# A spectral layer and an FFN: turning the first token block on PE instead of by DMA transposes, and a re-pipelined LayerNorm start

## The chip, the cores and the metric

The kernel runs on one core of a Trainium2 chip. The metric is the device time of one execution in microseconds (us). The engines are PE (TensorE, matmul; PEld is its weight load), DVE (VectorE), ACT (ScalarE), POOL (GpSimd) and SP (SyncE, which here issues DMAs). A profiled execution has a span, from its first to its last instruction; the time of the same execution is about 2 us longer.

## The reference, cut to what matters

```python
x = A_x                                              # 2048 tokens x 576
h  = x + irfft2(rfft2(layernorm(x)) * (w_r + 1j*w_i))  # A: spectral layer
h2 = h + (gelu(n @ w_gate) * (n @ w_up)) @ w_down      # B: FFN, n = layernorm(h), 4608 wide
```

## The kernel before

The kernel writes the transforms as matmuls with tables and goes through four parts: the start (LN1 and the first token transform), a loop of 16 steps (stages D, B and V: channel transform, product with W, and the way back), the inverse stage (I and N per token tile, residual, sums for LN2), and the FFN in four blocks of 512 tokens. gate/up contracts over 576 channels as 9 pieces of 64; gate uses rows 0 to 63 of the array and up rows 64 to 127 at the same time (the traces show about twice the columns per us: 648 matmuls of 512 columns in 70.1 us, where 10 of 289 columns that use all rows take 1.34 us). So it needs the normalised tokens turned (channels on partitions), with each 64-channel piece in both halves. Before, HN holds each piece twice, and nine 128x128 DMA transposes per token tile make HT from it.

A small recording layer takes operations in program order, each engine's list in order, and puts in the waits. In the traces here an engine (and the SP queue) stands at an operation that has to wait and does not go past it: in the run turn_dma20 below, the queue stands from 96.02 to 99.17 us before two copies.

```python
    # start: four rounds q of four token tiles; EPT is the epsilon tile
    P.op(POOL, lambda g: g.memset(EPT[:, :], EPS), w=["EPT"])   # stands behind 9 W loads on POOL
    def ln1_stats(q):
        ...  # 3 tiles by bn_stats on DVE, 1 tile by two ACT passes; sqrt on ACT (needs EPT), reciprocal on DVE
        for c in range(4 * q, 4 * q + 4):
            P.op(DVE, lambda v, c=c: v.tensor_scalar(ATS[:, c, :], ATB[:, c, :], RS1[:, c:c + 1], None, op0=ALU.mult), ...)
    for q in range(4):
        ln1_stats(q)
        for dt in range(5):
            a_mm(q, dt)
            if q >= 1:
                a_ev(q - 1, dt)          # odd dt on DVE, even dt on ACT
    ...
    def prep(c):                          # normalise tile c and turn it
        hs = c % 2                        # HN has two buffers
        for i in range(2):                # the 576 channels twice, in 64-wide pieces
            P.op(DVE, lambda v, ...: v.tensor_scalar(HN[:, hs, :, i, :], x9, TM[:, 1, c:c + 1], RS2[:, c:c + 1], ...), ...)
        for k in range(9):
            P.dma(SP, HT[:, k, 128 * (c % 4):128 * (c % 4) + 128], HN[:, hs, k, :, :]..., transpose=True)
    for c in range(NT + 1):               # inverse stage
        if c < NT: st_I(c)                # 10 matmuls
        if c >= 1: st_N(c - 1)            # 2 matmuls; residual on DVE, squares on ACT
        if c in (5, 9, 13): ln2((c - 5) // 4)
        if 5 <= c < 9: prep(c - 5)        # the first FFN block
    ...
    for tb in range(4):
        for f in range(36):
            gu(36 * tb + f, tb, f)        # 18 matmuls
            if tb < 3 and f % 4 == 3 and f < 16:
                prep(4 * (tb + 1) + f // 4)
        for p in range(4): down(tb, p)
```

Of the kernel before, what the change touches and what calls it, by code (L numbers as in the profile page):

```python
# [14 lines left out]
NG = 16  # L15
# [14 lines left out]
def build_tables():  # L30
# [95 lines left out]
    dt_[4, 64:96] = N[256:288]  # L126
    T["DTAB"] = dt_.transpose(1, 0, 2).reshape(128, -1)
# [154 lines left out]
def _build(nc, A_x, A_w_r, A_w_i, B_w_gate, B_w_up, B_w_down, out):  # L282
# [10 lines left out]
    HN = sb.alloc("HN", [128, 2, 9, 2, 64], BF16)  # L293
# [58 lines left out]

    P.op(POOL, lambda g: g.memset(WS[:, :, :, K2:KW], 0.0), w=["Wz"])
    xv = A_x[0].rearrange("(p c) d -> p c d", c=NT)
    ov = out[0].rearrange("(p c) d -> p c d", c=NT)
    for q in range(4):
        P.dma(SP, XO[:, 4 * q:4 * q + 4, :], xv[:, 4 * q:4 * q + 4, :], f"x{q}", w=[("X", c) for c in range(4 * q, 4 * q + 4)])
# [5 lines left out]
    for pl, src in ((0, A_w_r), (1, A_w_i)):  # L363
        eng = (SP, POOL)[pl]
        P.op(eng, None, r=[("X", 4)])
        for jj in range(4):
            a = bass.AP(src.tensor, 16 * jj * K2, [[128 * K2, 16], [K2, NG], [1, K2]])
            P.dma(eng, WS[jj:64:4, :, pl, 0:K2], a, f"w{pl}", r=["Wz"], w=[("W", pl, jj)])
            a = bass.AP(src.tensor, (64 + 16 * jj + 15) * K2, [[128 * K2, 16], [-K2, NG - 1], [1, K2]])
            P.dma(eng, WS[64 + jj:128:4, 1:NG, pl, 0:K2], a, f"w{pl}", r=["Wz"], w=[("W", pl, 4 + jj)])  # L370
        a = bass.AP(src.tensor, 64 * K2, [[128 * K2, 16], [16 * K2, 4], [1, K2]])
        P.dma(eng, WS[64:128, 0, pl, 0:K2], a, f"w{pl}", r=["Wz"], w=[("W", pl, 8)])
# [3 lines left out]
    P.dma(SP, IT[:, :, :].rearrange("p a b -> p (a b)"), dram["ITAB"][:, :], "it", w=["IT"])  # L376

    P.op(POOL, lambda g: g.memset(EPT[:, :], EPS), w=["EPT"])
    P.op(POOL, lambda g: g.memset(U[64:128, 4, :, :, :], 0.0), w=["Uz"])
# [4 lines left out]
    def ln1_stats(q):  # L384
        for c in range(4 * q, 4 * q + 4):
            if c % 4 == 3:
# [4 lines left out]
                continue  # L391
            for h in range(2):
                P.op(DVE, lambda v, c=c, h=h: v.bn_stats(ST1[:, c, h, :], XO[:, c, 288 * h:288 * h + 288]), r=[("X", c)], w=[("ST1", c, h)])  # L393
        for c in range(4 * q, 4 * q + 4):
            if c % 4 == 3:
# [4 lines left out]
            else:  # L400
                P.op(DVE, lambda v, c=c: v.bn_aggr(MV1[:, c, :], ST1[:, c, :, :]), r=[("ST1", c, 0), ("ST1", c, 1)], w=[("MV1", c)])
        cs = slice(4 * q, 4 * q + 4)
        P.op(ACT, lambda a, cs=cs: a.activation(RS1[:, cs], MV1[:, cs, 1], ACTF.Sqrt, bias=EPT[:, 0:1]),
             r=[("MV1", c) for c in range(4 * q, 4 * q + 4)] + ["EPT"], w=[("SD1", q)])
        P.op(DVE, lambda v, cs=cs: v.reciprocal(RS1[:, cs], RS1[:, cs]), r=[("SD1", q)], w=[("RS1", q)])
        for c in range(4 * q, 4 * q + 4):
            P.op(DVE, lambda v, c=c: v.tensor_scalar(ATS[:, c, :], ATB[:, c, :], RS1[:, c:c + 1], None, op0=ALU.mult),  # L407
                 r=[("RS1", q), "ATB"], w=[("ATS", c)])
# [10 lines left out]
    def a_ev(q, dt):  # L419
# [4 lines left out]
        if dt % 2 == 1:  # L424
# [4 lines left out]
    for q in range(4):  # L429
        ln1_stats(q)  # L430
        for dt in range(5):
            a_mm(q, dt)
            if q >= 1:
                a_ev(q - 1, dt)
    for dt in range(5):
        a_ev(3, dt)
# [77 lines left out]
    P.alias(["FT", "BT", "VT"], [("HT", 0, i) for i in range(4)])  # L514
# [14 lines left out]
    def st_N(c):  # L529
        sl = c % 2  # L530
        for h in range(2):
            b = 4 + 2 * sl + h
# [3 lines left out]
        P.op(DVE, lambda v, sl=sl, x2=x2, c=c: v.scalar_tensor_tensor(x2, banks(4 + 2 * sl, 2, 288), 1.0, x2, op0=ALU.mult, op1=ALU.add,  # L536
                                                                      accum_out=SB2[:, 0, c:c + 1]),
             r=[("PS", 4 + 2 * sl), ("PS", 5 + 2 * sl)], w=[("X", c), ("S0", c)])
# [3 lines left out]
    def ln2(q):  # L542
# [5 lines left out]
             r=[("M2", q)] + [("S1", c) for c in rr], w=[("V2", q)])  # L548
        P.op(ACT, lambda a, cs=cs: a.activation(RS2[:, cs], RS2[:, cs], ACTF.Sqrt, bias=EPT[:, 0:1]), r=[("V2", q), "EPT"], w=[("SD2", q)])
        P.op(DVE, lambda v, cs=cs: v.reciprocal(RS2[:, cs], RS2[:, cs]), r=[("SD2", q)], w=[("RS2", q)])  # L550

    def prep(c):
        hs = c % 2
        q = c // 4
        x9 = XO[:, c, :].rearrange("p (k e) -> p k e", e=64)
        for i in range(2):
            P.op(DVE, lambda v, c=c, hs=hs, i=i, x9=x9: v.tensor_scalar(HN[:, hs, :, i, :], x9, TM[:, 1, c:c + 1], RS2[:, c:c + 1],  # L557
                                                                        op0=ALU.subtract, op1=ALU.mult),
                 r=[("X", c), ("MN", q), ("RS2", q)], w=[("HN", hs, i)])
        HT = HTS[q % 2]  # L560
        for k in range(9):
            P.dma(SP, HT[:, k, 128 * (c % 4):128 * (c % 4) + 128], HN[:, hs, k, :, :].rearrange("p a b -> p (a b)"), f"tr{c}",
                  r=[("HN", hs, 0), ("HN", hs, 1)], w=[("HT", q % 2, c % 4)] if k == 8 else [("HTp", q % 2, c % 4, k)], transpose=True)

    for c in range(NT + 1):
        if c < NT:
# [3 lines left out]
        if c in (5, 9, 13):  # L570
            ln2((c - 5) // 4)
        if 5 <= c < 9:
            prep(c - 5)
    ln2(3)
# [80 lines left out]
```

## Time and profile before

The time is 569.71 us (median of four runs, 567.68 to 570.77). The profiled span is 565.9 us.

| part | from, us | length, us | bound by |
|---|---|---|---|
| start | 0 | 33.6 | DVE, after a late first round |
| D/B/V loop | 33.58 | 46.1 | PE |
| inverse stage and hand-over | 79.67 | 59.4 | the DMA transposes of the first block |
| FFN | 139.10 | 426.8 | PE |

These are three rows of the slice view of the kernel before: 40 slices of 14.1 us, each digit a busy share in tenths; PEclk is the clock granted to TensorE.

```profile
PE   0579987262999999999999999999999999999998
PEclk9999999556999999999999999999999999999999
DMA  8979998111011100001110000011100000000000
```

PE is full from the eleventh slice on. Before that lie a slow start and a hole in slices 8 to 10, where the granted clock is down to 0.5 and 0.6 as well (half clock, for short). The chain of waits of the same kernel says what held each (start in us, length, then engine, what it wrote, source line and number of instructions):

```profile
8.22 5.15 POOL WS L192 x9
...
13.56 1.28 ACT L403
14.85 0.31 ACT RS_55 L403
...
29.92 0.27 DVE ATS L407
30.23 2.63 PE PS L415 x20
...
33.58 4.99 PE PS L447 x20
...
79.67 2.61 PE PS L524 x20
...
111.87 1.23 SPq L190
113.15 2.33 DMA HT_68<-HN
...
129.51 9.59 issue
139.10 71.39 PE PS L590 x648
```

The first square root (L403) waits until 13.56 us, because EPT comes after nine W loads on POOL; the 1.28 us then are the load of its ACT table, and the square root itself follows at 14.85 us. In the hand-over the chain is the SP queue (SPq L190): 36 transposes, one every 1.27 us. The last 9.59 us are put down to "issue"; the gate/up matmuls (L590) then start when the last transposes have landed. The view by windows of the same stretch (busy us and, in brackets, instructions of each engine, then granted clock, DMA share and GB/s) shows PE starving:

```profile
core 0: us, PE busy (x) PEld busy (x) DVE busy (x) ACT busy (x) POOL busy (x), PEclk, DMA share, GB/s
90.00:100.00 10.00, 5.85 (x45) 4.00 (x43) 3.54 (x9) 3.36 (x9) 0.00 (x0) 1.00 0.73 237
100.00:110.00 10.00, 2.84 (x12) 1.64 (x12) 1.73 (x4) 1.31 (x3) 0.00 (x0) 0.54 0.13 26
110.00:120.00 10.00, 1.41 (x7) 0.74 (x7) 3.45 (x11) 2.38 (x7) 0.00 (x0) 0.50 0.13 28
120.00:130.00 10.00, 8.39 (x48) 5.47 (x46) 4.27 (x15) 6.65 (x16) 0.00 (x0) 0.77 0.11 23
130.00:140.00 10.00, 0.90 (x6) 0.43 (x8) 0.99 (x6) 2.36 (x4) 0.00 (x0) 0.58 0.11 23
```

The DMA share there is 0.11 to 0.13. The transposes load the engines little; they come slowly one after another.

### The profile page before, as it was taken

The page shows a single profiled execution, that of the slowest core. Times are in us where ns is not written, and L with a number is a line of the kernel's source. Part 1 is how long each engine was busy: PE and PEld are TensorE (multiplying, and loading weights), DVE is VectorE, ACT ScalarE, POOL GpSimd, SP SyncE. Part 2 cuts the span into 40 slices and gives each one's busy share as a digit, 9 for nine tenths or more (in the row PEclk, how much of TensorE's full clock was granted, in tenths as well). Part 3 has the DMA queues.
Part 4 walks back from the last instruction along what each step waited for, and adds up shares of the span by engine and source line. Part 5 has one row for each costly group of instructions (what it writes and reads, how often), then busy time and mean ns, then how long its engine had stood idle before and what let it go on. Part 6 is the DMA issues. An engine that isn't in the chain of part 4 may idle for free.

```text
span 565.9 us, 10092 instructions
## 1 busy us (share of the span) xinstructions
PE 506.5 (90%) x4368; PEld 300.5 (53%) x4368; DVE 192.8 (34%) x440; ACT 149.8 (26%) x279; POOL 27.7 (5%) x45
## 2 busy tenths in 40 slices
PE   0579987262999999999999999999999999999998
PEld 0457765141555557754444677444447754444676
DVE  1857754141444330025433210444330023333200
ACT  2545655043223220012233100332220012332100
POOL 4180040000000000000000000000000000000000
PEclk9999999556999999999999999999999999999999
DMA  8979998111011100001110000011100000000000
GB/s 316 230 169 221 222 237 294 26 26 21 8 27 27 25 4 17 17 12 22 24 27 15 6 17 22 11 24 27 24 3 17 17 12 1 1 2 1 6 21 17
DMA packets 35916, 31.37 MB, mean 55 GB/s; under 512 B 24433, under 2 KB 30705, under 8 KB 35873
## 3 DMA queue, kind: packets, MB, share of 16 engines
q0 software_dynamic: 4592, 17.11, 12.6%
q1 hardware_dynamic: 31136, 13.11, 9.0%
q8 instruction: 34, 0.56, 0.4%
q10 hardware_dynamic: 144, 0.52, 0.3%
q14 instruction: 10, 0.07, 0.0%
HBM read 23.64 MB, written 2.36 MB: 46 GB/s over the span
## 4 chain that ended last, share of the span: by engine, by line
PE 79%; SPq 7%; DVE 5%; issue 3%; DMA 2%; ACT 2%; POOL 1%; DVEq 0%; ACTq 0%
PE PS L590 44%; PE PS L603 25%; SPq L190 7%; PE PS L447 4%; PE PS L524 2%; PE PS L461 1%; DMA XO<-in_A_x_dram 1%; DVE ST_52 L393 1%; PE PS L480 1%; POOL WS L192 1%; DMA HT_68<-HN 1%; DVE XO L536 1%; DVE HN L557 1%; ACT SQ L539 1%; PE PS L533 1%
## 5 line engine op out<-in xcount | busy, mean ns | idle before, releaser
L594 ACT ACTIVATE GL<-PS 128x512 bf16<-128x512 f32 x144 | 86.0, 597 | 309.6 <-PE PS L590 306.4
L595 DVE TENSOR_TENSOR AT<-GL,PS 128x512 bf16<-128x512 bf16 x144 | 98.8, 687 | 174.6 <-ACT GL L594 174.4
L590 PE MATMUL PS<-HT_68,WGU 64*128 64x512 bf16 x1296 | 141.9, 378 | 9.8 <-issue 9.6
L603 PE MATMUL PS<-WD,AT 128*128 128x288 bf16 x1152 | 141.8, 286 | 0.0
L590 PE MATMUL PS<-HT_82,WGU 64*128 64x512 bf16 x1296 | 140.6, 376 | 0.1
L603 PEld LDWEIGHTS PS<-WD,AT 128*128 128x128 bf16 x1152 | 112.4, 98 | 29.9 <-issue 1.7
L590 PEld LDWEIGHTS PS<-HT_68,WGU 64*128 64x128 bf16 x1296 | 67.1, 95 | 84.1 <-issue 11.6
L590 PEld LDWEIGHTS PS<-HT_82,WGU 64*128 64x128 bf16 x1296 | 62.8, 94 | 77.4 <-DVE AT L595 0.6
L606 DVE TENSOR_TENSOR OS<-PS,XO 128x288 bf16<-128x288 f32 x32 | 14.6, 458 | 123.9 <-PE PS L603 123.9
L415 PE MATMUL PS<-ATS,XO 128*128 128x128 bf16 (+1 forms) x80 | 10.4, 309 | 22.5 <-DVE ATS L407 22.5
L557 DVE TENSOR_SCALAR HN<-XO,TM,RS_58 128x576 bf16<-128x576 bf16 x32 | 16.8, 567 | 28.5 <-DMA HT_68<-HN 23.0
L533 PE MATMUL PS<-GS,IT 128*128 128x288 bf16 x32 | 7.4, 318 | 21.0 <-ACT GS L526 21.0
L524 PE MATMUL PS<-DT,V 128*128 128x288 bf16 x160 | 25.7, 316 | 0.5 <-ACT V L487 0.5
L447 PE MATMUL PS<-FT,U 128*128 128x289 bf16 x160 | 24.7, 307 | 0.7 <-ACT U L427 0.7
L415 PEld LDWEIGHTS PS<-ATS,XO 128*128 128x128 bf16 (+1 forms) x80 | 8.0, 141 | 24.6 <-DVE ATS L407 23.2
L524 PEld LDWEIGHTS PS<-DT,V 128*128 128x128 bf16 x160 | 17.2, 108 | 6.5 <-issue 0.6
L447 PEld LDWEIGHTS PS<-FT,U 128*128 128x128 bf16 x160 | 15.4, 103 | 6.9 <-issue 0.9
L539 ACT ACTIVATE SQ<-XO 128x576 bf16<-128x576 bf16 x16 | 10.9, 681 | 26.0 <-DVE XO L536 26.0
L536 DVE SCALAR_TENSOR_TENSOR XO<-PS,XO 128x576 bf16<-128x576 f32 x16 | 12.0, 751 | 11.4 <-PE PS L533 11.4
L533 PEld LDWEIGHTS PS<-GS,IT 128*128 128x128 bf16 x32 | 3.0, 106 | 23.6 <-ACT GS L526 22.8
L480 PE MATMUL PS<-VT,ZS 128*128 128x256 bf16 x64 | 9.6, 271 | 2.1 <-DVE ZS L471 1.3
L393 DVE BATCH_NORM_STATS2 ST_52<-XO 128x6 f32<-128x288 bf16 x24 | 9.0, 445 | 6.5 <-DMA XO<-in_A_x_dram 6.5
(50 smaller groups left out, 170.1 us busy)
## 6 DMA issues: line engine op xcount, KB each, us to landing
WGU<-in_B_w_gate_dram POOLq DMA_DIRECT2D x9, 576.0 KB, 22.2
WGU<-in_B_w_up_dram POOLq DMA_DIRECT2D x9, 576.0 KB, 24.1
WD<-in_B_w_down_dram POOLq DMA_DIRECT2D x9, 576.0 KB, 10.5
XO<-in_A_x_dram SPq DMA_DIRECT2D x4, 576.0 KB, 7.2
out_dram<-OS SPq DMA_DIRECT2D x32, 72.0 KB, 1.6
HT_68<-HN SPq DMA_TRANSPOSE x72, 2.4
HT_82<-HN SPq DMA_TRANSPOSE x72, 2.4
FT<-c_ftab SPq DMA_DIRECT2D x1, 725.0 KB, 9.6
```

The source lines that it names most:

```text
L190: fn = lambda e: e.dma_start(out_ap, in_ap, transpose=True)
L415: P.op(PE, lambda t, b=b, w=w, i=i, c=c, dt=dt: t.matmul(bank(b, 0, w, 128 * i, 128 * i + 128), XO[:, c, 128 * dt:128 * dt + w], ATS[:, c, ...
L447: P.op(PE, lambda t, b=b, o=o, dt=dt, g=g: t.matmul(bank(b, 0, 128, 0, K2), U[:, dt, g, :, :], FT[:, dt, o, 0:K2], start=(dt == 0), stop=( ...
L524: P.op(PE, lambda t, b=b, h=h, kt=kt, c=c: t.matmul(bank(b, 0, 128, 0, 288), V[:, kt, c, :, :], DT[:, kt, 288 * h:288 * h + 288], start=(k ...
L533: P.op(PE, lambda t, b=b, h=h, c=c, sl=sl: t.matmul(bank(b, 0, 128, 0, 288), IT[:, c, :], GS[:, sl, 288 * h:288 * h + 288], start=True, st ...
L536: P.op(DVE, lambda v, sl=sl, x2=x2, c=c: v.scalar_tensor_tensor(x2, banks(4 + 2 * sl, 2, 288), 1.0, x2, op0=ALU.mult, op1=ALU.add, accum_o ...
L539: P.op(ACT, lambda a, sl=sl, c=c: a.activation(SQ[:, sl, :], XO[:, c, :], ACTF.Square, accum_out=SB2[:, 1, c:c + 1]), r=[("X", c)], w=[("S ...
L557: P.op(DVE, lambda v, c=c, hs=hs, i=i, x9=x9: v.tensor_scalar(HN[:, hs, :, i, :], x9, TM[:, 1, c:c + 1], RS2[:, c:c + 1], op0=ALU.subtract ...
L590: P.op(PE, lambda t, o=o, h0=h0, kt=kt, f=f, b0=b0, HT=HT: t.matmul(bank(b0 + o), WGU[h0:h0 + 64, kt, 128 * f:128 * f + 128], HT[h0:h0 + 6 ...
L594: P.op(ACT, lambda a, s2=s2, b0=b0: a.activation(GL[:, s2, :], bank(b0), ACTF.Gelu_apprx_tanh), r=[("PS", b0)], w=[("GL", s2)])
L595: P.op(DVE, lambda v, s2=s2, b0=b0, f=f: v.tensor_tensor(AT[:, f, :], GL[:, s2, :], bank(b0 + 1), op=ALU.mult), r=[("GL", s2), ("PS", b0 + ...
L603: P.op(PE, lambda t, b0=b0, h=h, f=f, p=p: t.matmul(bank(b0 + h, 0, 128, 0, 288), AT[:, f, 128 * p:128 * p + 128], WD[:, f, 288 * h:288 * ...
```

## The change

There are two intents. In the inverse stage, the first block is turned by five PE matmuls per tile with an identity matrix, copied out of PSUM by DVE, and the other four slots are filled by two half-shifted SBUF copies by DMA. HN now holds each piece once, plus one repeated piece. In the start, the LN1 statistics, the scaling (now one operation on POOL per round) and the PSUM evacuations are spread over DVE, ACT and POOL, EPT is set first, x comes in smaller pieces, and all W loads move to SP. Blocks 2 to 4 of the FFN keep their DMA transposes.

```diff
-    HN = sb.alloc("HN", [128, 2, 9, 2, 64], BF16)
+    HN = sb.alloc("HN", [128, 2, 640], BF16)
+    IDT = sb.alloc("IDT", [128, 128], BF16)
...
+    P.op(POOL, lambda g: g.memset(EPT[:, :], EPS), w=["EPT"])          # now first on POOL
-    for q in range(4):                                                 # x in 4 pieces
+    for i, (c0, c1) in enumerate(((0, 2), (2, 4), (4, 8), (8, 12), (12, 16))):
-        eng = (SP, POOL)[pl]                                           # W loads
+            P.dma(SP, WS[jj:64:4, :, pl, 0:K2], a, f"w{pl}", ...)
...
-        for c in range(4 * q, 4 * q + 4):
-            P.op(DVE, lambda v, c=c: v.tensor_scalar(ATS[:, c, :], ATB[:, c, :], RS1[:, c:c + 1], ...
+        P.op(POOL, lambda g, cs=cs: g.tensor_tensor(ATS[:, cs, :], ATB[:, cs, :], RS1[:, cs].unsqueeze(2).to_broadcast([128, 4, 128]), op=ALU.mult), ...
...
+    ln1_act(0); ln1_stats(0); ln1_sqrt(0)                              # one per line in the kernel
+    ln1_act(1); ln1_stats(1); ln1_scale(0); ln1_sqrt(1)
+    a_quad(0, (ACT, ACT, ACT, ACT, ACT))                               # matmuls and evacuations
+    ln1_act(2); ln1_stats(2); ln1_scale(1); ln1_sqrt(2)
+    a_quad(1, (ACT, ACT, DVE, ACT, DVE))
+    ln1_act(3); ln1_stats(3); ln1_scale(2); ln1_sqrt(3)
+    a_quad(2, (ACT, DVE, ACT, DVE, DVE))
+    ln1_scale(3)
+    a_quad(3, (ACT, DVE, ACT, DVE, ACT))
...
+    def turn_pe(c):
+        for k in range(5):
+            P.op(PE, ... t.matmul(bank(b, 0, 128, o, o + 128), HN[:, hs, 128 * k:128 * k + 128], IDT[:, :], start=True, stop=True), ...)
+        P.op(DVE, ... v.tensor_copy(HT0[:, 0:5, t0:t1], PS[:, 6 * 512:6 * 512 + 640]...), ...)
+        P.dma(SP, HT0[0:64, 5:9, t0:t1], HT0[64:128, 0:4, t0:t1], f"tr{c}", ...)
+        P.dma(SP, HT0[64:128, 5:9, t0:t1], HT0[0:64, 1:5, t0:t1], f"tr{c}", ...)
...
-        if 5 <= c < 9:
-            prep(c - 5)
+        if c in (6, 8, 10, 12):
+            norm((c - 6) // 2)
+        if c in (7, 9, 11, 13):
+            turn_pe((c - 7) // 2)
...
+    GT = (0, 5, 1, 6, 2, 7, 3, 8, 4)      # slot of piece kt for gate
+    UT = (4, 0, 5, 1, 6, 2, 7, 3, 8)      # and for up
```

N uses one pair of PSUM banks in place of two, since banks 6 and 7 now take the turned tiles, and the steps of LN2 are spread over neighbouring tiles (cut here). a_quad(q, engines) is the five matmuls of a round with their evacuations, one engine named for each.

More of the change, by code (lines that the diff above doesn't have):

```diff
@@ L126, in build_tables @@
     dt_[4, 64:96] = N[256:288]
+    T["EYE"] = np.eye(128)
     T["DTAB"] = dt_.transpose(1, 0, 2).reshape(128, -1)
@@ L350, in banks @@
         return PS[:, b * 512:(b + n) * 512].rearrange("p (a c) -> p a c", a=n)[:, :, 0:w]
+    P.op(POOL, lambda g: g.memset(EPT[:, :], EPS), w=["EPT"])
     P.op(POOL, lambda g: g.memset(WS[:, :, :, K2:KW], 0.0), w=["Wz"])
+    P.op(POOL, lambda g: g.memset(U[64:128, 4, :, :, :], 0.0), w=["Uz"])
     xv = A_x[0].rearrange("(p c) d -> p c d", c=NT)
     ov = out[0].rearrange("(p c) d -> p c d", c=NT)
-    for q in range(4):
-        P.dma(SP, XO[:, 4 * q:4 * q + 4, :], xv[:, 4 * q:4 * q + 4, :], f"x{q}", w=[("X", c) for c in range(4 * q, 4 * q + 4)])
+    for i, (c0, c1) in enumerate(((0, 2), (2, 4), (4, 8), (8, 12), (12, 16))):
+        P.dma(SP, XO[:, c0:c1, :], xv[:, c0:c1, :], f"x{i}", w=[("X", c) for c in range(c0, c1)])
     P.dma(ACT, ATB[:, :, :].rearrange("p a b -> p (a b)"), dram["ATAB"][:, :], "atb", w=["ATB"])
@@ L363, in _build @@
     for pl, src in ((0, A_w_r), (1, A_w_i)):
-        eng = (SP, POOL)[pl]
-        P.op(eng, None, r=[("X", 4)])
         for jj in range(4):
             a = bass.AP(src.tensor, 16 * jj * K2, [[128 * K2, 16], [K2, NG], [1, K2]])
-            P.dma(eng, WS[jj:64:4, :, pl, 0:K2], a, f"w{pl}", r=["Wz"], w=[("W", pl, jj)])
+            P.dma(SP, WS[jj:64:4, :, pl, 0:K2], a, f"w{pl}", r=["Wz"], w=[("W", pl, jj)])
             a = bass.AP(src.tensor, (64 + 16 * jj + 15) * K2, [[128 * K2, 16], [-K2, NG - 1], [1, K2]])
-            P.dma(eng, WS[64 + jj:128:4, 1:NG, pl, 0:K2], a, f"w{pl}", r=["Wz"], w=[("W", pl, 4 + jj)])
+            P.dma(SP, WS[64 + jj:128:4, 1:NG, pl, 0:K2], a, f"w{pl}", r=["Wz"], w=[("W", pl, 4 + jj)])
         a = bass.AP(src.tensor, 64 * K2, [[128 * K2, 16], [16 * K2, 4], [1, K2]])
-        P.dma(eng, WS[64:128, 0, pl, 0:K2], a, f"w{pl}", r=["Wz"], w=[("W", pl, 8)])
+        P.dma(SP, WS[64:128, 0, pl, 0:K2], a, f"w{pl}", r=["Wz"], w=[("W", pl, 8)])
     GORD = list(range(1, NG)) + [0]
@@ L376, in _build, with ln1_act @@
     P.dma(SP, IT[:, :, :].rearrange("p a b -> p (a b)"), dram["ITAB"][:, :], "it", w=["IT"])
-    P.op(POOL, lambda g: g.memset(EPT[:, :], EPS), w=["EPT"])
-    P.op(POOL, lambda g: g.memset(U[64:128, 4, :, :, :], 0.0), w=["Uz"])
+    P.dma(SP, IDT[:, :], dram["EYE"][:, :], "eye", w=["IDT"])
     P.op(POOL, lambda g: g.memset(YS[:, :, :, K2:KW], 0.0), w=["Yz"])
     P.op(POOL, lambda g: g.memset(ZS[:, :, :, K2:ZW], 0.0), w=["Zz"])
-    def ln1_stats(q):
+    ACT_TILES = (1, 5, 9, 13)
+    def ln1_act(q):
         for c in range(4 * q, 4 * q + 4):
-            if c % 4 == 3:
+            if c in ACT_TILES:
                 P.op(ACT, lambda a, c=c: a.activation(JNK[:, 0, :], XO[:, c, :], ACTF.Identity, accum_out=SA[:, 0, c:c + 1]),
@@ L390, in ln1_stats @@
                      r=[("X", c)], w=[("SA1", c), "J1"])
-                continue
-            for h in range(2):
-                P.op(DVE, lambda v, c=c, h=h: v.bn_stats(ST1[:, c, h, :], XO[:, c, 288 * h:288 * h + 288]), r=[("X", c)], w=[("ST1", c, h)])
+    def ln1_stats(q):
         for c in range(4 * q, 4 * q + 4):
-            if c % 4 == 3:
+            if c not in ACT_TILES:
+                for h in range(2):
+                    P.op(DVE, lambda v, c=c, h=h: v.bn_stats(ST1[:, c, h, :], XO[:, c, 288 * h:288 * h + 288]), r=[("X", c)], w=[("ST1", c, h)])
+        for c in range(4 * q, 4 * q + 4):
+            if c not in ACT_TILES:
+                P.op(DVE, lambda v, c=c: v.bn_aggr(MV1[:, c, :], ST1[:, c, :, :]), r=[("ST1", c, 0), ("ST1", c, 1)], w=[("MV1", c)])
+        for c in range(4 * q, 4 * q + 4):
+            if c in ACT_TILES:
                 P.op(DVE, lambda v, c=c: v.scalar_tensor_tensor(TM[:, 0, c:c + 1], SA[:, 0, c:c + 1], 1.0 / (D * D), SA[:, 0, c:c + 1],
@@ L399, in ln1_stats, with ln1_sqrt @@
                                                                 op0=ALU.mult, op1=ALU.subtract), r=[("SA1", c), ("TM", c)], w=[("MV1", c)])
-            else:
-                P.op(DVE, lambda v, c=c: v.bn_aggr(MV1[:, c, :], ST1[:, c, :, :]), r=[("ST1", c, 0), ("ST1", c, 1)], w=[("MV1", c)])
+    def ln1_sqrt(q):
         cs = slice(4 * q, 4 * q + 4)
@@ L404, in ln1_stats, with ln1_scale @@
              r=[("MV1", c) for c in range(4 * q, 4 * q + 4)] + ["EPT"], w=[("SD1", q)])
+    def ln1_scale(q):
+        cs = slice(4 * q, 4 * q + 4)
         P.op(DVE, lambda v, cs=cs: v.reciprocal(RS1[:, cs], RS1[:, cs]), r=[("SD1", q)], w=[("RS1", q)])
-        for c in range(4 * q, 4 * q + 4):
-            P.op(DVE, lambda v, c=c: v.tensor_scalar(ATS[:, c, :], ATB[:, c, :], RS1[:, c:c + 1], None, op0=ALU.mult),
-                 r=[("RS1", q), "ATB"], w=[("ATS", c)])
+        P.op(POOL, lambda g, cs=cs: g.tensor_tensor(ATS[:, cs, :], ATB[:, cs, :], RS1[:, cs].unsqueeze(2).to_broadcast([128, 4, 128]), op=ALU.mult),
+             r=[("RS1", q), "ATB"], w=[("ATS", c) for c in range(4 * q, 4 * q + 4)])
     def a_mm(q, dt):
@@ L417, in a_mm, with a_ev @@
                  r=[("X", c), ("ATS", c)], w=[("PS", b)])
-    def a_ev(q, dt):
+    def a_ev(q, dt, eng):
         b = (5 * q + dt) % 8
@@ L423, in a_ev @@
         dst = U[0:w, dt, :, 4 * q:4 * q + 4, :].rearrange("p g n e -> p n g e")
-        if dt % 2 == 1:
+        if eng == DVE:
             P.op(DVE, lambda v, s=src, d=dst: v.tensor_copy(d, s), r=[("PS", b)], w=[("U", q, dt)])
@@ L427, in a_ev, with a_quad @@
             P.op(ACT, lambda a, s=src, d=dst: a.activation(d, s, ACTF.Copy), r=[("PS", b)], w=[("U", q, dt)])
-    for q in range(4):
-        ln1_stats(q)
+    def a_quad(q, engs):
         for dt in range(5):
             a_mm(q, dt)
-            if q >= 1:
-                a_ev(q - 1, dt)
-    for dt in range(5):
-        a_ev(3, dt)
+            a_ev(q, dt, engs[dt])
+    ln1_act(0)
+    ln1_stats(0)
+    ln1_sqrt(0)
+    ln1_act(1)
+    ln1_stats(1)
+    ln1_scale(0)
+    ln1_sqrt(1)
+    a_quad(0, (ACT, ACT, ACT, ACT, ACT))
+    ln1_act(2)
+    ln1_stats(2)
+    ln1_scale(1)
+    ln1_sqrt(2)
+    a_quad(1, (ACT, ACT, DVE, ACT, DVE))
+    ln1_act(3)
+    ln1_stats(3)
+    ln1_scale(2)
+    ln1_sqrt(3)
+    a_quad(2, (ACT, DVE, ACT, DVE, DVE))
+    ln1_scale(3)
+    a_quad(3, (ACT, DVE, ACT, DVE, ACT))
     ukeys = [("U", q, dt) for q in range(4) for dt in range(5)] + ["Uz"]
@@ L513, in _build @@
         P.dma(POOL, WD[:, 4 * j:4 * j + 4, :], wdv[:, 4 * j:4 * j + 4, :], f"wd{j}", w=[("WD", j)])
-    P.alias(["FT", "BT", "VT"], [("HT", 0, i) for i in range(4)])
+    P.alias(["FT", "BT", "VT"], [("HT", 0, i, k) for i in range(4) for k in range(3)])
     vkeys = [("V", g) for g in range(NG)] + [("Vt", g) for g in range(NG)]
@@ L531, in st_N @@
         for h in range(2):
-            b = 4 + 2 * sl + h
+            b = 4 + h
             P.op(PE, lambda t, b=b, h=h, c=c, sl=sl: t.matmul(bank(b, 0, 128, 0, 288), IT[:, c, :], GS[:, sl, 288 * h:288 * h + 288], start=True, stop=True),
@@ L535, in st_N, with ln2_a @@
         x2 = XO[:, c, :].rearrange("p (a b) -> p a b", a=2)
-        P.op(DVE, lambda v, sl=sl, x2=x2, c=c: v.scalar_tensor_tensor(x2, banks(4 + 2 * sl, 2, 288), 1.0, x2, op0=ALU.mult, op1=ALU.add,
-                                                                      accum_out=SB2[:, 0, c:c + 1]),
-             r=[("PS", 4 + 2 * sl), ("PS", 5 + 2 * sl)], w=[("X", c), ("S0", c)])
+        P.op(DVE, lambda v, x2=x2, c=c: v.scalar_tensor_tensor(x2, banks(4, 2, 288), 1.0, x2, op0=ALU.mult, op1=ALU.add,
+                                                               accum_out=SB2[:, 0, c:c + 1]),
+             r=[("PS", 4), ("PS", 5)], w=[("X", c), ("S0", c)])
         P.op(ACT, lambda a, sl=sl, c=c: a.activation(SQ[:, sl, :], XO[:, c, :], ACTF.Square, accum_out=SB2[:, 1, c:c + 1]),
              r=[("X", c)], w=[("SQ", sl), ("S1", c)])
-    def ln2(q):
+    def ln2_a(q):
         cs = slice(4 * q, 4 * q + 4)
@@ L548, in ln2, with ln2_b, ln2_c, norm @@
              r=[("M2", q)] + [("S1", c) for c in rr], w=[("V2", q)])
+    def ln2_b(q):
+        cs = slice(4 * q, 4 * q + 4)
         P.op(ACT, lambda a, cs=cs: a.activation(RS2[:, cs], RS2[:, cs], ACTF.Sqrt, bias=EPT[:, 0:1]), r=[("V2", q), "EPT"], w=[("SD2", q)])
+    def ln2_c(q):
+        cs = slice(4 * q, 4 * q + 4)
         P.op(DVE, lambda v, cs=cs: v.reciprocal(RS2[:, cs], RS2[:, cs]), r=[("SD2", q)], w=[("RS2", q)])
-    def prep(c):
+    def norm(c):
         hs = c % 2
         q = c // 4
-        x9 = XO[:, c, :].rearrange("p (k e) -> p k e", e=64)
-        for i in range(2):
-            P.op(DVE, lambda v, c=c, hs=hs, i=i, x9=x9: v.tensor_scalar(HN[:, hs, :, i, :], x9, TM[:, 1, c:c + 1], RS2[:, c:c + 1],
-                                                                        op0=ALU.subtract, op1=ALU.mult),
+        for i, (o0, o1, x0, x1) in enumerate(((0, D, 0, D), (D, 640, 0, 64))):
+            P.op(DVE, lambda v, c=c, hs=hs, o0=o0, o1=o1, x0=x0, x1=x1: v.tensor_scalar(HN[:, hs, o0:o1], XO[:, c, x0:x1], TM[:, 1, c:c + 1],
+                                                                                        RS2[:, c:c + 1], op0=ALU.subtract, op1=ALU.mult),
@@ L559, in prep, with turn_dma @@
                  r=[("X", c), ("MN", q), ("RS2", q)], w=[("HN", hs, i)])
+    def turn_dma(c):
+        hs = c % 2
+        q = c // 4
         HT = HTS[q % 2]
         for k in range(9):
-            P.dma(SP, HT[:, k, 128 * (c % 4):128 * (c % 4) + 128], HN[:, hs, k, :, :].rearrange("p a b -> p (a b)"), f"tr{c}",
-                  r=[("HN", hs, 0), ("HN", hs, 1)], w=[("HT", q % 2, c % 4)] if k == 8 else [("HTp", q % 2, c % 4, k)], transpose=True)
+            o = 128 * k if k < 5 else 64 + 128 * (k - 5)
+            P.dma(SP, HT[:, k, 128 * (c % 4):128 * (c % 4) + 128], HN[:, hs, o:o + 128], f"tr{c}",
+                  r=[("HN", hs, 0), ("HN", hs, 1)], w=[("HT", q % 2, c % 4, k)], transpose=True)
@@ new lines, in turn_pe @@
+    def turn_pe(c):
+        hs = c % 2
+        t0, t1 = 128 * c, 128 * c + 128
+        for k in range(5):
+            b, o = 6 + k // 4, 128 * (k % 4)
+            P.op(PE, lambda t, b=b, o=o, k=k, hs=hs: t.matmul(bank(b, 0, 128, o, o + 128), HN[:, hs, 128 * k:128 * k + 128], IDT[:, :], start=True, stop=True),
+                 r=[("HN", hs, 0), ("HN", hs, 1), "IDT"], w=[("PS", b)])
+        P.op(DVE, lambda v, t0=t0, t1=t1: v.tensor_copy(HT0[:, 0:5, t0:t1], PS[:, 6 * 512:6 * 512 + 640].rearrange("p (k e) -> p k e", k=5)),
+             r=[("PS", 6), ("PS", 7)], w=[("HT", 0, c, 0)])
+        P.dma(SP, HT0[0:64, 5:9, t0:t1], HT0[64:128, 0:4, t0:t1], f"tr{c}", r=[("HT", 0, c, 0)], w=[("HT", 0, c, 1)])
+        P.dma(SP, HT0[64:128, 5:9, t0:t1], HT0[0:64, 1:5, t0:t1], f"tr{c}", r=[("HT", 0, c, 0)], w=[("HT", 0, c, 2)])
@@ L565, in _build @@
     for c in range(NT + 1):
+        if c in (6, 10, 14):
+            ln2_b((c - 6) // 4)
         if c < NT:
@@ L570, in _build @@
         if c in (5, 9, 13):
-            ln2((c - 5) // 4)
-        if 5 <= c < 9:
-            prep(c - 5)
-    ln2(3)
+            ln2_a((c - 5) // 4)
+        if c in (6, 10, 14):
+            ln2_c((c - 6) // 4)
+        if c in (6, 8, 10, 12):
+            norm((c - 6) // 2)
+        if c in (7, 9, 11, 13):
+            turn_pe((c - 7) // 2)
+    ln2_a(3)
+    ln2_b(3)
+    ln2_c(3)
     fdead = vkeys + ["DT", "IT", ("G", 0), ("G", 1), ("Y", 0), ("Y", 1), "Yz", "Zz", ("SQ", 0), ("SQ", 1)]
     fdead += [("T1", a) for a in range(2)] + [(n_, a, b_) for n_ in ("T2", "Z") for a in range(2) for b_ in range(2)]
-    P.alias(fdead, [("AT", f) for f in range(36)] + [("GL", 0), ("GL", 1)] + [("HT", 1, i) for i in range(4)] +
-            [("HTp", 1, i, k) for i in range(4) for k in range(9)])
-    P.alias(["FT", "BT", "VT"], [("HTp", 0, i, k) for i in range(4) for k in range(9)])
+    P.alias(fdead, [("AT", f) for f in range(36)] + [("GL", 0), ("GL", 1)] + [("HT", 1, i, k) for i in range(4) for k in range(9)])
+    GT = (0, 5, 1, 6, 2, 7, 3, 8, 4)
+    UT = (4, 0, 5, 1, 6, 2, 7, 3, 8)
     def gu(n, tb, f):
@@ L585, in gu @@
         HT = HTS[tb % 2]
-        rk = [("HT", tb % 2, i) for i in range(4)] + [("WG", f // 4, i) for i in range(2)]
+        rk = [("HT", tb % 2, i, k) for i in range(4) for k in range(9)] + [("WG", f // 4, i) for i in range(2)]
         for kt in range(9):
             for o in range(2):
-                h0 = 64 * o
-                P.op(PE, lambda t, o=o, h0=h0, kt=kt, f=f, b0=b0, HT=HT: t.matmul(
-                    bank(b0 + o), WGU[h0:h0 + 64, kt, 128 * f:128 * f + 128], HT[h0:h0 + 64, kt, :], start=(kt == 0), stop=(kt == 8)),
+                h0, sl = 64 * o, (GT, UT)[o][kt]
+                P.op(PE, lambda t, o=o, h0=h0, kt=kt, sl=sl, f=f, b0=b0, HT=HT: t.matmul(
+                    bank(b0 + o), WGU[h0:h0 + 64, kt, 128 * f:128 * f + 128], HT[h0:h0 + 64, sl, :], start=(kt == 0), stop=(kt == 8)),
                     r=rk, w=[("PS", b0 + o)])
@@ L614, in _build @@
             if tb < 3 and f % 4 == 3 and f < 16:
-                prep(4 * (tb + 1) + f // 4)
+                norm(4 * (tb + 1) + f // 4)
+                turn_dma(4 * (tb + 1) + f // 4)
         for p in range(4):
```

## The prediction

> **What bounds the kernel now.** The page gives a span of 565.9 us, PE busy 90%. By the chain of waits and the timeline: (1) Start, 0 to 33.6 us: LN1 and the first transform; the chain runs through DVE (rounds of about 5.2 us: statistics 2.16, scaling 0.74, evacuations 1.2), after a first round that waits until 13.5 us for the EPT memset, which stands on POOL behind nine W loads (5.15 us). (2) D/B/V loop, 33.6 to 79.7 us, PE-bound at 2.51 us per step. (3) Inverse stage and hand-over, 79.7 to 139.1 us: PE needs only 1.47 us per tile (1.23+0.24), 23.5 us for 16, but 36 DMA transposes are issued 1.27 us apart from 92 us on. DVE (HN, two buffers) stalls behind them, PE starves, and its granted clock falls to 0.50-0.58 between 100 and 120 us. The last 9.6 us, shown as "issue", are gate/up waiting for the last transposes. (4) FFN, 139.1 us to the end, 426.8 us: PE-bound, 4 x (70.0 to 71.4 + 35.4).
>
> **What the change does.**
> - Inverse stage: removes the 36 transposes; adds 20 PE matmuls (about 0.12 us each, as in the first transform: 2.5 us), four PSUM copies of 640 columns (about 0.8 us, from 0.6 us for 512) on DVE, and eight half-shift DMAs (estimate 2 to 5 us each, beside the W_down load). DVE and ACT stay below PE's pace: DVE 0.78 per tile plus 0.7 or 0.8 on alternate tiles, ACT about 1.33. N now has one bank pair, with about 0.45 us slack. Expected stage: 23.5 + 2.5 + last latency 0.9 + stalls up to 1 = 27 to 28 us for 59.4: **31 to 32 us gained**, all on the critical path. PE doesn't idle, so no half clock: the Trainium skill ("TensorE: Matmul & The Clock Gate", Part 1) says idling PE falls to half clock; the granted 0.50 agrees. That gives another 1 us in the first gate/up block.
> - Start: EPT no longer waits and X comes in smaller pieces, so round 0 starts about 5 us earlier. But the rounds become a serial loop over engines: statistics of round 2 wait for ACT, which first evacuates all of round 0; scaling sits on POOL. "GPSIMD Engine Reference" § 3.1 gives about 2.6 cycles per element for two inputs; for 512 elements I estimate 1.1 to 1.3 us, four times in the chain, for 0.74 on DVE (no run shows it yet). Adding up: scaling of rounds 0 to 3 ends at 12.5, 19, 27, 32; loop start about **34.5 us (32 to 37)** for 33.6. So the start gains nothing, perhaps loses 1 us.
> - W loads all move to SP: later end (27 to 36 us), needed at about 41: no stall. Weight loads start some us later, still long before use.
> - FFN: same matmuls, slots permuted: no change; blocks 1-3 keep DMA transposes, which don't stall PE.
>
> **Sum.** 565.9 - 31.5 - 1.2 + 0.9 = 534 us span; the time 569.6 - 32 = **537.5 us** (range 531 to 543). Faster by over 2%: 0.98; within 2%: 0.015; slower: 0.005.
>
> **What would show it.** No transposes before gate/up; first gate/up matmul near 108 us; granted clock 1.0 throughout; PE over 95% busy in the inverse stage; D loop still 2.51 us per step; first D matmul at 32 to 37 us with DVE idle behind ACT or POOL; FFN 425 to 426 us.
>
> **What would make it wrong.** POOL scaling far from 1.2 us (each 0.5 us is 2 us of start); W landing after 41 us; half-shift copies slow under the W_down load, so gate/up waits; N stalling on its single bank pair; a slower gate/up from the permuted slots.

## The result, and the profile after

The time is 533.01 us (median of four runs, 532.34 to 533.64). The ratio to before is 0.936, with a 95% interval of 0.933 to 0.9389. Ratios here are the mean time of one kernel's fast runs over that of the other's of the same rounds, so not quite the ratio of the quoted medians. The span of the profiled run is 530.8 us.

| part | before, us | after, us | gained |
|---|---|---|---|
| start, to the first D matmul | 33.58 | 33.15 | 0.4 |
| D/B/V loop | 46.09 | 46.02 | 0.1 |
| inverse stage and hand-over | 59.43 | 27.24 | 32.2 |
| first gate/up block | 71.39 | 70.11 | 1.3 |
| the rest | 355.4 | 354.3 | 1.1 |

The slice view of the changed kernel, the same three rows, shows no hole any more:

```profile
PE   0379989999999999999999999999999999999997
PEclk9999999999999999999999999999999999999999
DMA  8979999401110000011100000111000000000000
```

Its chain of waits, the start and the hand-over:

```profile
5.59 2.26 DVE ST_53 L399 x6
...
11.33 1.04 POOL ATS L418
...
13.06 2.52 ACT U L438 x5
...
17.27 1.04 POOL ATS L418
...
24.41 1.05 POOL ATS L418
...
28.87 1.05 POOL ATS L418
29.97 2.47 PE PS L426 x20
...
33.15 4.99 PE PS L475 x20
...
79.17 2.61 PE PS L552 x20
...
104.04 2.13 DMA HT_69<-HT_69
106.41 70.11 PE PS L649 x648
```

The first round starts about 4 us earlier (POOL scaling at 11.33 us, where DVE scaled at 15.47 us before), and nearly all of it is given back: scaling comes 5.9, 7.1 and 4.5 us apart, and the chain passes through POOL and ACT as well as DVE. In the hand-over nothing but one half-shift copy of 2.13 us stands before gate/up. By windows PE is now nearly full through the stage, at full clock:

```profile
90.00:100.00 10.00, 9.66 (x85) 7.26 (x84) 8.52 (x27) 8.24 (x20) 0.00 (x0) 1.00 0.80 256
100.00:110.00 10.00, 8.62 (x76) 5.39 (x76) 6.07 (x21) 8.09 (x18) 0.00 (x0) 1.00 0.11 26
110.00:120.00 10.00, 10.00 (x96) 5.24 (x92) 4.68 (x8) 3.03 (x6) 0.00 (x0) 1.00 0.04 8
```

### The profile page after: what moved, and what is told of

Read it like the earlier page. It is cut to its first block, busy times and chain, and to the rows that moved or that the text cites. A ratio compares the mean times of both kernels' runs of the same rounds, so it can differ in the third digit from the quotient of the medians.

```text
span 530.8 us, 10113 instructions
## 1 busy us (share of the span) xinstructions
PE 500.6 (94%) x4388; PEld 301.1 (57%) x4388; DVE 185.9 (35%) x427; ACT 151.1 (28%) x280; POOL 26.8 (5%) x40
## 3 DMA queue, kind: packets, MB, share of 16 engines
q0 software_dynamic: 4176, 15.93, 12.5%
## 4 chain that ended last, share of the span: by engine, by line
PE 91%; DVE 4%; DMA 1%; ACT 1%; POOL 1%; issue 0%; SPq 0%; DVEq 0%; POOLq 0%
PE PS L649 53%; PE PS L662 27%; PE PS L475 4%; PE PS L552 3%; PE PS L426 1%; PE PS L489 1%; DVE ST_53 L399 1%; PE PS L508 1%; DMA XO<-in_A_x_dram 1%; POOL ATS L418 1%; ACT U L438 1%; PE PS L512 1%; DVE XO L564 1%; PE PS L561 0%; DMA HT_69<-HT_69 0%
## 5 line engine op out<-in xcount | busy, mean ns | idle before, releaser
L662 PEld LDWEIGHTS PS<-WD,AT 128*128 128x128 bf16 x1152 | 112.4, 98 | 29.9 <-issue 1.7
L552 PE MATMUL PS<-DT,V 128*128 128x288 bf16 x160 | 22.0, 286 | 0.5 <-ACT V L515 0.5
L552 PEld LDWEIGHTS PS<-DT,V 128*128 128x128 bf16 x160 | 15.4, 98 | 4.3 <-issue 0.6
L590 DVE TENSOR_SCALAR HN<-XO,TM,RS_59 128x576 bf16<-128x576 bf16 (+1 forms) x32 | 10.2, 360 | 7.3 <-DMA HT_83<-HN 5.3
L481 ACT ACTIVATE CUS<-PS 128x289 bf16<-128x289 f32 x16 | 6.6, 414 | 16.7 <-PE PS L475 16.7
L494 DVE TENSOR_TENSOR T_78<-YS,WS 128x580 bf16<-128x580 bf16 x16 | 7.4, 461 | 11.0 <-ACT YS L492 11.0
L489 PE MATMUL PS<-CUS,BT 128*128 128x289 bf16 x64 | 11.1, 296 | 0.1
```

The lines of the kernel that those rows point to most:

```text
L489: P.op(PE, lambda t, b=b, o=o, tb=tabs[o], sl=sl, sp_=sp_: t.matmul(bank(b, 0, 128, 0, K2), BT[:, sp_, tb, :], CUS[:, sl, o, 0:K2], start= ...
L552: P.op(PE, lambda t, b=b, h=h, kt=kt, c=c: t.matmul(bank(b, 0, 128, 0, 288), V[:, kt, c, :, :], DT[:, kt, 288 * h:288 * h + 288], start=(k ...
L662: P.op(PE, lambda t, b0=b0, h=h, f=f, p=p: t.matmul(bank(b0 + h, 0, 128, 0, 288), AT[:, f, 128 * p:128 * p + 128], WD[:, f, 288 * h:288 * ...
```

## The experiments

The theory (A) is that the gain is the 36 transposes taken off the path and nothing else. Rivals are that the pipelined start is worth several us of its own (B), and that what cost the time was the stall of DVE behind two HN buffers with the half clock that followed, not the transposes (C). The table lists all 11 runs. First D is the first matmul of the loop, where the start ends; first gate/up is where the hand-over ends. Both columns are read from the chain of waits of each run's one profiled execution. Each ratio is to the kernel before in the same rounds, whose median was 568.85 to 569.71 us.

| run | median, us | ratio to before | first D, us | first gate/up, us |
|---|---|---|---|---|
| before | 569.71 | 1 | 33.58 | 139.10 |
| the change | 533.01 | 0.936 | 33.15 | 106.41 |
| inv_only | 533.79 | 0.938 | 33.74 | 107.49 |
| start_only | 568.28 | 0.9985 | 33.08 | 138.60 |
| hn4 | 569.73 | 1.0014 | 33.65 | 140.35 |
| turn_dma20 | 558.25 | 0.981 | 33.20 | 129.58 |
| turn_dma20b | 553.35 | 0.9731 | 32.98 | 122.69 |
| ept_first | 563.12 | 0.9907 | 28.27 | 133.16 |
| scale_dve | 529.74 | 0.9328 | 31.18 | 103.22 |
| reorder | 528.18 | 0.9278 | 22.58 | 99.66 |
| gate_wd | 522.19 | 0.918 | 22.52 | 95.80 |
| gate_dve | 525.04 | 0.9221 | 24.86 | 99.50 |
| best | 520.32 | 0.9152 | 21.17 | 94.93 |

### Each half alone: inv_only and start_only

inv_only is the changed kernel with the old start section put back (and the identity load kept); start_only is the kernel before with the new start section put in.

> The old start with the new inverse stage. Theory A (the whole gain comes from taking the 36 transposes off the path; the new start is worth at most 1 us): 533 to 534.5 us, first D matmul at about 33.6 us as before, first gate/up matmul about 27.2 us after the first inverse matmul. Rival B (the pipelined start is worth several us of its own): 537 us or more.

> The new start with the old inverse stage and its 36 transposes. Theory A: 568 to 570 us, same as before within 0.3%; first D matmul at about 33.2 us; the hand-over still takes 59 us. Rival B: 565 us or less.

inv_only took 533.79 us and start_only 568.28 us (ratio 0.9985, interval 0.9959 to 1.0011). By the medians of the same rounds, the new inverse stage alone gives 35.3 us of the whole change's 36.7, the new start alone 0.8 us, which its interval does not tell from noise. Rival B falls. Start and inverse stage add up; neither hides the other. One expectation was missed: inv_only's inverse stage took 28.7 us, not 27.2, and 1.4 us of the excess lies in its first 20 matmuls (4.05 us for 2.61), partly at half clock.

### Was it the transposes, or the stall behind two buffers? hn4

```diff
-    HN = sb.alloc("HN", [128, 2, 9, 2, 64], BF16)
+    HN = sb.alloc("HN", [128, 3, 9, 2, 64], BF16)
...
-        hs = c % 2
+        hs = c if c < 4 else c % 2
+        HB = HN[:, hs] if hs < 3 else OS...   # the fourth buffer lies in the output staging tile
```

> The kernel before with four HN buffers for the first block in place of two (the fourth lies in the output staging tile, unused until then), so that DVE never waits for a transpose; same 36 transposes. Theory A (what counts is the 36 transposes, one after another at 1.27 us each from about 91.5 us on): PE finishes the inverse stage near 105 us at full clock, then idles; gate/up still starts at 138 to 139 us; total within 1.5 us of before. Rival C (what counts is the stall of DVE behind two buffers and the half clock that follows): gate/up starts 10 us or more earlier, total below 560 us.

It took 569.73 us, the same as before (569.12 us in its rounds). The timeline of PE in this run shows why (start, length, engine, line, operation; in brackets the idle time before it and what ended it):

```profile
107.29 0.42 PE L533 MATMUL PS<-GS,IT 128*128 128x288 bf16 x2 [1.12 <-ACT GS L526]
140.35 1.04 PE L593 MATMUL PS<-HT,WGU 64*128 64x512 bf16 x4 [32.64 <-DMA HT<-OS]
```

With DVE free, PE finishes the inverse stage at 107.7 us, where it needed until 129.5 us before, and then waits 32.6 us for the last transpose. Gate/up starts at 140.35 us, 1.4 us later than the expected range and not 10 us earlier. Rival C falls: the stall and the half clock inside the stage were not on the path; the queue of transposes was.

### Fewer transposes: turn_dma20 and turn_dma20b

turn_dma20 is the changed kernel with five DMA transposes per tile in place of the PE matmuls and the DVE copy; the half-shift copies stay.

> The changed kernel, but its first block is turned by 5 DMA transposes per tile (20 in all) in place of PE matmuls; the half-shift copies stay. Theory A: 20 transposes at 1.27 us plus the last landing and half-shift copy: from about 91 us, gate/up starts at 118 to 123 us against 106.4, so 545 to 550 us in all. If the number of transposes did not matter and any use of the transposing DMA cost the old price, it would be near 565 us; if the PE turn were not needed, near 533 us.

It took 558.25 us, 8 us more than the top of the expected range. The timeline of the SP queue in this run:

```profile
89.74 6.28 SPq L191 DMA_TRANSPOSE HT<-HN  x5
99.17 1.35 SPq L193 DMA_DIRECT2D HT<-HT  x2
100.57 6.35 SPq L191 DMA_TRANSPOSE HT<-HN  x5
108.08 1.25 SPq L193 DMA_DIRECT2D HT<-HT  x2
```

The five transposes take the expected 1.27 us each, but the copies read what they wrote, so the queue, which is in order, stands until the last has landed, and the next tile's transposes stand behind it. The period is about 9.1 us (99.17 to 126.57 us for three tiles, by the same timeline), not the 6.4 of five issues. turn_dma20b issues each tile's copies after the next tile's transposes:

```diff
         if c in (7, 9, 11, 13):
             turn_pe((c - 7) // 2)          # here: the five transposes only
+        if c in (9, 11, 13):
+            half((c - 9) // 2)             # the two copies of the tile before
+    half(3)
```

> As the run with 20 DMA transposes, but each tile's two half-shift copies are issued after the next tile's transposes. In that run (558 us) the queue stood still after each tile for the last landing (2.4 us) before it could issue the copies (1.3 us), and DVE waited as well: 9.4 us per tile in place of 6.4. Theory: with the order changed the 20 transposes go at 1.27 us each from about 90 us to 116 us, the last landing and copies add 5 us, gate/up starts at 120 to 123 us, total 549 to 552 us. Rival (copies and transposes hinder each other in the DMA engines): stays near 558 us.

Gate/up started at 122.69 us, within the expected 120 to 123 us, and the profiled run took 551.82 us; the median, 553.35 us, lies 1.4 us above the range. The expectation had left out that PE comes back at half clock: its first gate/up block took 72.68 us for 70.11. So the hand-over's cost follows the number of transposes and the waits put into their queue, and theory A holds through 36, 20 and 0 transposes.

### Why the start gained nothing: ept_first and scale_dve

ept_first is the kernel before with the EPT memset moved to the head of POOL, one line.

> The kernel before with one line moved: the memset of EPT is the first instruction of POOL. Theory: the first square root comes at about 9.4 us in place of 14.85, the rounds keep their 5.2 us pace, first D matmul at about 28 us for 33.6, total 563 to 565 us. Rival (the start waits for data: X, W or tables; or the gain is lost to later waits): 568 us or more.

It took 563.12 us, with the first D matmul at 28.27 us. The chain of waits shows the first square root at 8.81 us, where it stood at 14.85 us before:

```profile
8.81 0.30 ACT RS L403
...
9.43 0.74 DVE ATS L407 x4
...
28.27 4.33 PE PS L447 x20
```

One moved line is worth 5.7 us of the medians of its rounds (568.85 us before). The changed kernel contains the same line and is at 33.15 us, so the rest of its new start cost about 4.9 us (33.15 less 28.27).

scale_dve is the changed kernel with the scaling given back to DVE:

```diff
-        P.op(POOL, lambda g, cs=cs: g.tensor_tensor(ATS[:, cs, :], ATB[:, cs, :], ...
+        for c in range(4 * q, 4 * q + 4):
+            P.op(DVE, lambda v, c=c: v.tensor_scalar(ATS[:, c, :], ATB[:, c, :], RS1[:, c:c + 1], ...
```

> The changed kernel with its LN1 scaling back on DVE (four 128x128 per round) in place of one POOL operation. In the two traces it takes 0.5 to 0.7 us from the start of the reciprocal to the first matmul with DVE, and 1.34 to 1.41 us with POOL, four times in the chain. Theory: first D matmul at 30 to 30.5 us for 33.15, total about 3 us less, 529.5 to 530.5 us. Rival (DVE is what bounds the start, so POOL relieves it): 533 us or more.

It took 529.74 us, but the start moved less than expected: first D matmul at 31.18 us, 2.0 us earlier, not 3. The trace's other 1.2 us to gate/up (103.22 for 106.41) came in the D loop, whose first 20 matmuls took 4.15 us in place of 4.99 us. Ten such matmuls take 1.34 us later in the loop, so these still run at about half rate for part of the time (though the granted clock of that stretch reads 1.00), and when that ends varies from run to run. So POOL scaling explains about 2 us of the 4.9.

### The order of the start: reorder

The changed kernel with another program order in its start. The statistics stand ahead of the evacuations on both engines; mm(q) and ev(q, ...) are the two halves of a_quad. The expectation calls this a change of order only, but the edit also moves two of round 1's evacuations from DVE to ACT (DVE has 5 in place of 7, at about 0.69 us each). The new lines, several to a line and without those they replace:

```diff
+    ln1_act(0); ln1_stats(0); ln1_sqrt(0); ln1_act(1); ln1_act(2); ln1_scale(0); mm(0)
+    ln1_stats(1); ln1_sqrt(1); ln1_act(3); ln1_scale(1); ev(0, (0, ACT), (1, ACT), (2, ACT))
+    ln1_stats(2); ln1_sqrt(2); ev(0, (3, ACT), (4, ACT)); mm(1)
+    ln1_scale(2); ev(1, (0, ACT), (1, ACT), (2, ACT))
+    ln1_stats(3); ln1_sqrt(3); ev(1, (3, ACT), (4, ACT)); mm(2)
+    ln1_scale(3); ev(2, (0, DVE), (1, ACT), (2, DVE), (3, ACT), (4, DVE))
     a_quad(3, (ACT, DVE, ACT, DVE, ACT))
```

> The changed kernel with only the program order of its start altered: the ACT statistics of rounds 2 and 3 stand ahead of the evacuations of round 0, the DVE statistics of a round stand ahead of DVE evacuations of the round before, scaling stays on POOL. Theory (the start of the changed kernel is slow because its in-order engines form one serial loop, not because any engine is full): DVE becomes the bound at about 3.1 us a round, first D matmul at 22.5 to 24.5 us, total 523 to 526 us. Rival (X or W arrives too late, or DVE has no room): first D matmul or first product with W held until 32 us or more, total 530 us or more.

The start came as expected: first D matmul at 22.58 us, 10.6 us earlier, with the rounds 3.2 us apart. The end of its start in the chain of waits:

```profile
15.07 2.14 DVE ST L399 x6
...
18.30 1.05 POOL ATS L418
19.40 2.47 PE PS L426 x20
...
22.58 4.44 PE PS L488 x20
```

Apart from the two moved evacuations (about 1.4 us of DVE time) the same engines do the same work on the same data, so most of the 10.6 us is the order: the start after the change was slow mainly because of it. The two were not tested apart. But the total, 528.18 us, missed its range (only one of its four executions, 523.93 us, lies inside). The chain of waits at the hand-over shows where some of the gain went:

```profile
93.33 0.59 SPq L193
...
93.96 5.45 DMA HT<-HT
...
99.66 3.57 PE PS L662 x15
```

The last half-shift copy took 5.45 us, where it took 2.13 us in the changed kernel. By the view of the HT tile, PE waited 3.7 us for it; after that the first gate/up block ran partly at half clock and took 72.79 us. The DMA engines were full until about 96 us (344 GB/s between 85 and 95 us, by the view of windows): the W_down load, which in the changed kernel was over by about 98 us, before the last copies. The prediction had named this as a risk for the change itself. There the first two copies did take 5.1 and 5.8 us under the end of the load, but nothing waited for them, and the last four, issued after it, took 2.1 us (view of the DMA issues). Once the start was faster, the load ran beside the last copy too, and PE waited.

### The W_down load out of the way: gate_wd

```diff
+    P.op(POOL, None, r=[("HT", 0, i, k) for i in range(4) for k in (1, 2)])   # after the inverse stage
     for j in range(9):
         P.dma(POOL, WD[:, 4 * j:4 * j + 4, :], wdv[:, 4 * j:4 * j + 4, :], f"wd{j}", w=[("WD", j)])
```

> As the run reorder (528.2 us), but the W_down load waits until the eight half-shift copies of the first block have landed. In reorder the first D matmul came 10.6 us earlier than in the changed kernel, but gate/up only 6.8 us earlier: PE stood 3.7 us before gate/up for the last copy, which took 5.5 us under the W_down load, and the first gate/up block then ran partly at half clock (72.8 for 70.1 us). Theory: without the load beside them the copies land in about 2.3 us, gate/up starts 26.5 to 28.5 us after the first inverse matmul, at 94 to 96 us, and the first block takes 70 to 70.5 us: total 521 to 523.5 us. Rival (the copies are slow for another reason, or W_down then comes too late for the first down block): 527 us or more, or a wait before the first down matmul.

It took 522.19 us (ratio 0.918, interval 0.916 to 0.9201). The same place in its chain of waits:

```profile
92.78 0.59 SPq L193
...
93.41 2.15 DMA HT<-HT
...
95.80 1.24 PE PS L664 x9
```

The copy is back at 2.15 us, the inverse stage takes 27.3 us as in the changed kernel, and the first gate/up block 70.16 us. Nothing waits for W_down later: the chain shows gate/up and down back to back. The Trainium skill ("DMA: Bandwidth & Descriptors", section "Queues, rings and completion order") says that each DMA engine goes round its queues a packet at a time, so a small copy shares with a large load on another queue. The two durations here, 5.45 us beside the load and 2.15 us without it, agree; no run here tells this sharing from another way in which the load could slow the copy.

### POOL or DVE for the scaling, once the order is right: gate_dve, and best

gate_dve is gate_wd with the scaling on DVE, the edit of scale_dve.

> As gate_wd, with the LN1 scaling on DVE (four 128x128 per round, 0.74 us) in place of POOL. In the changed kernel's own order DVE scaling saved 3 us, because DVE stood idle there. Theory: in the new order DVE is the bound, so three rounds of 0.74 us ahead of the later statistics are added and the last round saves about 0.85: first D matmul at 23.5 to 24.5 us for 22.6, total 1 to 2 us more than gate_wd. Rival (POOL scaling is always the slower choice): 1 us or more below gate_wd.

It took 525.04 us, 2.8 us more than gate_wd (intervals 0.9199 to 0.9243 and 0.916 to 0.9201, which just touch; all five executions lie above all four of gate_wd), first D matmul at 24.86 us for 22.52. The direction was right, but both figures lie above the expected 1 to 2 us and 23.5 to 24.5 us. The start explains 2.3 us; in the profiled run the first 20 inverse matmuls were also partly at half clock (4.28 us for 2.61), as in some other runs, so the 2.8 us is not all scaling. The same edit that gained 2.0 us of start in the one order loses 2.3 us in the other. In the order of the change DVE stood idle around the scaling; in the new order DVE is the bound, and one POOL operation of 1.04 us runs beside it.

best is gate_wd with the statistics of one tile of the next round ahead of each reciprocal, and the last round's scaling on DVE.

> As gate_wd, with the statistics of one tile of the next round ahead of each reciprocal (DVE stood 0.37 us per round for the square root) and the last round's scaling on DVE. Theory: first D matmul at 20.5 to 21.5 us; W, whose last copies are issued near 19 us and land near 28, may then hold the first product with W by up to 1.5 us, so total 0.5 to 2 us below gate_wd. Rival (W already bounds the start): no gain at all over gate_wd.

It took 520.32 us (ratio 0.9152, interval 0.9131 to 0.9173), 1.9 us below gate_wd, first D matmul at 21.17 us. The trace puts the waits of the first product with W down to ACT, none to a DMA, so W did not bind. The intervals of best and gate_wd overlap a little, so this last step is likely rather than certain. All outputs were correct in all runs.

## Why the prediction was right

The measured 533.0 us lies in the range of 531 to 543 us, 4.5 us below the predicted 537.5 us, and the mechanism was the one described.

- **Inverse stage.** Predicted 27 to 28 us, measured 27.24 us; the gain of 32.2 us is just above the predicted 31 to 32. hn4 and the pair with 20 transposes show that the queue of transposes was the cause. Inside the sum, a PE turn took 0.45 us per tile, 1.8 us in all for the predicted 2.5; the four PSUM copies took 0.82 us each for 0.8; the half-shift copies took 2.1 to 5.8 us (median 2.3) for the predicted 2 to 5, the slow ones where nothing waited for them. Gate/up waited 0.4 us for the last of them. PE was busy 25.53 of 27.24 us, 94%, where the prediction said over 95%.
- **Half clock.** "The granted clock 1.0 throughout" and "another 1 us in the first gate/up block": the profiled run has 1.0 and a gain of 1.3 us. The Trainium skill's statement ("TensorE: Matmul & The Clock Gate", Part 1) that an idle PE falls to half clock agrees with 0.50 in the old hole.
- **Start.** Predicted 34.5 us (32 to 37), measured 33.15 us; "gains nothing" is what start_only measured. The reasons held too: the scaling of the four rounds ended at 12.4, 18.3, 25.5 and 29.9 us for the predicted 12.5, 19, 27 and 32. One term that was too large is the POOL operation, 1.04 us for the estimated 1.1 to 1.3; four times, that is at most 1 us of the 2.1 by which the last scaling ended early, and the prediction does not break down the rest. From there to the first D matmul it left 2.5 us, and it took 3.2. The table load of the square root also ran before its input was ready, at 7.04 us. The prediction did name the serial loop over the engines; what it did not say is that another order would break it, for about 10 us.
- **FFN.** "No change; blocks 1-3 keep DMA transposes, which don't stall PE" was wrong by 1.1 us, and the FFN took 424.4 us for the predicted 425 to 426. Before, the second and third blocks took 105.92 and 105.99 us, after it 105.42 us both. In the second block of the kernel before, DVE waited 3.0 us for an HN buffer, then normalised for 1.05 us; ACT was held up by DVE and PE stood for 0.6 us before a weight load. After, DVE waited 2.0 us and normalised for 0.64 us, and neither ACT nor PE waited for it. That the shorter normalisation is the reason is read from the traces and was not tested alone.
- **The 4.5 us.** The gains between the two profiled spans add up to 35.1 us, where the prediction's terms add up to 31.8: the start was 1.3 us better than predicted, the inverse stage 0.7, the FFN after its first block 1.1. The rest lies between profiled runs and medians, which differ by 36.7 us: the profiled run of the kernel before (568.0 us) was 1.7 us below its median, that of the changed kernel only 0.4 us.

## What to carry to other kernels

Small DMA transposes in a row cost their issue time each (1.27 us here), even at a DMA share of 0.11 to 0.13; when PE has to wait for them anyway, matmuls with an identity and one PSUM copy can be far cheaper (0.45 us of PE and 0.82 us of DVE per tile here, and two copies by DMA). On in-order engines, decide the program order before deciding which engine gets an operation: the same move to POOL lost 2 us in one order and gained over 2 us in another. And when a stage gets faster, look at which background load it now runs into; a load that is needed late can be made to wait.

## What the Trainium skill lacked or had wrong

- "DMA: Bandwidth & Descriptors" has no figure for a 128x128 SBUF-to-SBUF DMA transpose on trn2 issued one by one. ("VectorE: DVE Perf Modes", section "The three transpose paths", does give 1309 ns for one by DMA and 390 ns on TensorE, so the figure is not missing from the skill.) Here SP issued them 1.27 us apart and the last landed 2.3 to 2.4 us after its issue; 36 in a row kept the queue for about 46 us (36 times 1.27) at a DMA share of 0.11 to 0.13. The DMA page's table of rules recommends the hardware transpose for a transpose during DMA; for tiles already in SBUF the page names TensorE only as an alternative, and here that was 0.45 us of PE per tile against 11.4 us of queue (9 times 1.27).
- "TensorE: Matmul & The Clock Gate", Part 1, gives an idle window of about 3.4 us as what brings the half clock. In some runs it came after shorter gaps (the same Part says of another kernel that PE idling briefly between groups of matmuls made the clock go back and forth, but not how long the gaps were): in reorder the gaps before the inverse stage were 0.8, 0.6 and 0.5 us, the granted clock between 65 and 70 us was 0.73, and the first 20 matmuls took 4.10 us for 2.61. The timeline of PE in that run shows the last two gaps in brackets:

```profile
66.27 0.60 PE L521 MATMUL PS<-VT,ZS 128*128 128x256 bf16 x4 [0.61 <-DVE ZS L512]
67.60 4.10 PE L565 MATMUL PS<-DT,V 128*128 128x288 bf16 x20 [0.50 <-ACT V L528]
```

  It is there in the profiled runs of inv_only (4.05 us), hn4 (4.22 us), gate_dve (4.28 us) and best (4.22 us) and not in those of before, of the change or of gate_wd (2.61 us), so it may be part of the spread of 1 to 3 us between executions; that it is was not shown.
- "GPSIMD Engine Reference", section 3.1, gives about 2.6 cycles per element for two inputs. The 512-element product took 1.04 us with its dispatch, 2.4 cycles per element at the page's 1.2 GHz, so it roughly agrees. Its section 4.1 sends elementwise work to VectorE; here POOL was the better choice by 2.3 us of start once DVE was the bound (gate_wd against gate_dve).
- No page that was read gives the cost of a small SBUF copy beside a large load: 2.15 us alone and 5.45 us beside the W_down load for the last of them; the first two of reorder, with the load in full flow, took 9.3 and 12.5 us, and in the changed kernel the four issued between 91 and 98 us had a median of 4.3 us, the four after that 2.1 us.
